# A transformer block on one core: part of VectorE's integer shifts goes to GpSimd, and two shifts become one pass

## The chip, the core and the metric

The kernel runs on one core of a Trainium2 chip. The core has a matrix engine (TensorE, PE in the profile; PEld is its weight loading), a vector engine (VectorE, DVE), an activation engine (ScalarE, ACT), a general engine (GpSimd, POOL) and a queue that issues transfers (SyncE, SP). Each engine works through its own list of instructions in order, and waits on semaphores for the others. PE writes its results to a memory of its own, PSUM; VectorE and ScalarE read PSUM, GpSimd in this kernel works on the main on-chip memory (SBUF) alone. The metric is the device time of one execution in microseconds.

## The reference

The input is one sequence of 2048 tokens of width 512, in bf16. A condition vector `c` gives six modulation vectors. Two branches follow, each with a layer norm and a residual:

```python
mod = (_silu(c) @ w_mod).reshape(c.shape[0], 6, 1, -1)
...
h = _layernorm(x) * (1 + ca) + sa
x = x + ga * attention(h, wqkv, wo)      # 32 heads of width 16, softmax over 2048 keys
h = _layernorm(x) * (1 + cb) + sb
x = x + gb * (gelu(h @ w1 + b1) @ w2 + b2)   # hidden width 1376
```

Nearly all the time is in the attention: 32 heads x 2048 x 2048 scores, of which every one has to be turned into an exponential.

## The kernel before

**Two ways to an exponential.** The queries are taken in four blocks of 512 (`QB`), the heads in four groups of eight; a run is four heads of one group for one block, and there are 32 runs (`NR`). A run has 16 key tiles of 128 keys. A unit is one head, one key tile, 512 queries: a 128 x 512 tile of scores in PSUM.

- *ScalarE's way.* `qk_a` puts three or two units (in turn) into a PSUM tile `st`, and line 847 makes the exponential of 1536 or 1024 columns into `pt` with one instruction.
- *VectorE's way.* `qk_d` computes one unit at a time into `ax`, and line 895 evicts it: it adds a constant, clamps at zero and writes a 16-bit integer into a quarter of the tile `ph` (four units: 2048 columns). Read as bf16, such an integer is already a rough exponential, piecewise linear. `shifts` (line 912) adds four further constants (`PH_SH`) to the 2048 integers, one VectorE pass each into a tile `sh` (line 915). The bf16 readings of all five, summed, approximate the exponential far better. The sum is not made: `pv_op` lets PE multiply each of the five readings with the values and add them up in PSUM (`od`), so a key tile on this way costs five such products instead of one.

In each run but the first, the key tiles 2, 6, 10 and 14 (`DKS`) are meant for VectorE; when ScalarE has finished its own tiles of a run, `next_tile` hands it what VectorE has not begun.

**Who sets the order.** All instructions are ordered by a planner (`Plan`) while the program is built. An `Op` has an engine, a duration that the planner assumes, a delay until its result can be used, a priority, operations it waits for, and a buffer it takes (`acq`, a `Res` with so many slots) or gives back (`rel`). The planner goes through time, picks for each engine what can start first, and by priority among what can start at nearly the same time. A small random number (`spread`) is added to the priority; its seed is taken from `SEEDS`, one for each 12.5 us of planned time. The order in which operations are picked is the order in each engine's list; on the chip only that order and the semaphores remain.

**GpSimd beside PSUM passes.** GpSimd multiplies the attention output with the reciprocal of its sum (`normalise`, line 1001; the sums go through SP's transfers to be spread over rows) and scales three weight tiles (`scaled`, line 1024). These are cut in two halves of 256 columns by `beside` (line 1032). The gate `plan.beside` lets such a piece start only next to a VectorE instruction that reads PSUM (`port=False`); `after_dve` makes it wait, on the chip, for the VectorE instruction ahead of that one. The flag `port=True` marks VectorE and GpSimd operations that the planner does not run at the same time.

**Start and end.** `load_x`, `load_mod` and `load_cols` issue SP's first loads: the first block of x in two halves, two modulation tiles, the first columns of the weights, which wait for the first modulation tile. `mod_columns`, `layer_norm`, `make_k`, `make_v`, `make_q` lead to the first scores. `make_q` is called ahead of need by `want_q`, with a due time. `block_tail` and `last_half` hold the output projection and the second branch of each block; the last block is done in two halves.

## Time and profile before

| | us |
|---|---|
| median of three runs | 786.2 (785.47 to 786.65) |
| the profiled execution | 786.85 |
| its span in the profile | 785.1 |
| ScalarE busy | 758.5 |
| VectorE busy | 729.0 |
| PE busy | 728.4 |
| GpSimd busy | 101.3 |
| exponentials, 632 instructions (line 847) | 716.6 |
| evictions to integers, 468 passes (line 895) | 307.7 |
| shifts, 468 passes (line 915) | 309.2 |

The clock granted to TensorE was 1.00 throughout. "Busy" counts the time in which at least one instruction of an engine was under way; successive passes of VectorE overlap by some 0.08 us in the records, so the mean duration of one (681 ns for an eviction) is longer than its share of the busy time (307.7 / 468 = 657 ns). The idle time of an engine costs nothing where another engine is the bound.

### The profile page before, as it was taken

To read this page: it belongs to the slowest core of one execution; us is meant where nothing else is said; L and a number is where in the kernel's file an instruction comes from. 1 tells how busy PE (TensorE), PEld (TensorE's weight loads), DVE (VectorE), ACT (ScalarE), POOL (GpSimd) and SP (SyncE) were. 2 spreads that over 40 slices of the span, in tenths; PEclk is the share of its full clock that TensorE was granted. 3 is DMA by queue.
4 is the path that set the end of the run, shared out by engine and by line. 5 is a ranking of instruction groups with operands and counts; after the bars stand their busy time and mean duration, and the time that the engine had idled before them with its cause. 6 is when DMAs were issued, how large, how long until landed. Compare 5 with 4: busy or idle time off the path is not lost.

```text
span 785.1 us, 20128 instructions
## 1 busy us (share of the span) xinstructions
PE 728.4 (93%) x8182; PEld 275.3 (35%) x8254; DVE 729.0 (93%) x1269; ACT 758.5 (97%) x686; POOL 101.3 (13%) x167
## 2 busy tenths in 40 slices
PE   8899999999999999999999999999888899989997
PEld 3433333333333222333233333222333444434444
DVE  6878899999999999999999999988999999999984
ACT  4999999999999999999999999999999999999994
POOL 6200103100002520010002100010001100120100
PEclk9999999999999999999999999999999999999999
DMA  7052001100011001001001010011010001000010
GB/s 215 30 168 59 18 24 43 26 15 15 15 45 49 25 19 49 18 19 44 10 20 33 24 32 7 17 33 30 25 45 24 18 18 43 20 24 18 25 44 28
DMA packets 39070, 28.19 MB, mean 36 GB/s; under 512 B 17957, under 2 KB 34374, under 8 KB 38978
## 3 DMA queue, kind: packets, MB, share of 16 engines
q1 hardware_dynamic: 38970, 26.91, 12.2%
q8 instruction: 64, 1.05, 0.6%
q14 instruction: 28, 0.23, 0.1%
q10 hardware_dynamic: 8, 0.00, 0.0%
HBM read 21.30 MB, written 2.61 MB: 30 GB/s over the span
## 4 chain that ended last, share of the span: by engine, by line
ACT 50%; PE 27%; issue 11%; DVE 10%; SPq 1%; DMA 1%; POOL 1%; POOLq 0%; DVEq 0%; ACTq 0%
ACT pt L847 47%; PE od L949 9%; PE st L798 8%; DVE sh L915 3%; DVE ph L895 3%; PE ax L1112 2%; PE ax L798 2%; ACT g L1191 1%; PE ax L1172 1%; PE ax L688 1%; SPq L716 1%; PE ax L428 1%; DVE g L1182 1%; PE t L1112 1%; PE ax L1106 0%
## 5 line engine op out<-in xcount | busy, mean ns | idle before, releaser
L847 ACT ACTIVATE pt<-st 128x1536 bf16<-128x1536 f32 x632 | 716.6, 1358 | 2.8 <-PE st L798 1.8
L895 DVE TENSOR_SCALAR ph<-ax 128x512 int16<-128x512 f32 x468 | 307.7, 681 | 15.3 <-PE ax L798 13.7
L915 DVE TENSOR_SCALAR sh<-ph 128x2048 int16<-128x2048 int16 x468 | 309.2, 691 | 2.0 <-PE od L949 1.3
L798 PE MATMUL st<-qm,kT 32*128 32x512 bf16 x1580 | 247.5, 382 | 28.9 <-ACT pt L847 22.5
L949 PE MATMUL od<-sh,VEB 128*32 128x512 bf16 (+1 forms) x2368 | 172.3, 339 | 5.4 <-DVE sh L915 3.4
L949 PEld LDWEIGHTS <-VEB 128*32 128x32 bf16 x4928 | 111.9, 95 | 161.8 <-issue 137.6
L798 PEld LDWEIGHTS <-kT 32*128 32x128 bf16 x2048 | 84.8, 91 | 235.8 <-issue 225.1
L798 PE MATMUL ax<-qm,kT 32*128 32x512 bf16 x468 | 159.8, 379 | 6.0 <-DVE ph L895 4.4
L949 PE MATMUL od<-pt,VEB 128*32 128x512 bf16 (+1 forms) x1968 | 153.6, 341 | 0.4 <-DVE OD L974 0.2
L1001 POOL TENSOR_TENSOR OT<-OD,RB 128x256 bf16<-128x256 f32 x38 | 27.9, 741 | 348.5 <-DVE sh L915 331.8
L949 PE MATMUL od<-ph,VEB 128*32 128x512 bf16 (+1 forms) x592 | 45.0, 337 | 0.0
L1172 PE MATMUL ax<-blk,W 128*128 128x512 bf16 (+1 forms) x143 | 39.5, 358 | 1.6 <-issue 0.8
L1001 POOL TENSOR_TENSOR OS<-OD,RB 128x256 bf16<-128x256 f32 x24 | 17.1, 727 | 174.8 <-DVE sh L915 154.9
L688 PE MATMUL ax<-blk,w 128*128 128x512 bf16 x100 | 32.5, 383 | 3.9 <-ACT blk L610 1.4
L1112 PE MATMUL ax<-w,g 128*128 128x512 bf16 x103 | 29.3, 381 | 1.6 <-DVE ph L895 0.8
L1182 DVE TENSOR_SCALAR g<-ax,b1c 128x512 bf16<-128x512 f32 (+1 forms) x41 | 28.3, 691 | 0.3
L594 DVE BATCH_NORM_STATS2 ln_s<-xb 128x6 f32<-128x512 bf16 x32 | 21.7, 677 | 1.2 <-DMA xb<-in_A_x_dram 1.1
L1112 PEld LDWEIGHTS <-g 128*128 128x128 bf16 x176 | 14.4, 97 | 22.3 <-issue 10.5
L974 DVE COPY OD<-od 128x512 f32<-128x512 f32 x31 | 21.2, 683 | 1.0 <-PE od L949 0.8
L1172 PEld LDWEIGHTS <-W 128*128 128x128 bf16 x176 | 13.4, 97 | 21.0 <-issue 15.5
L727 PE MATMUL ax<-w,blk 128*128 128x128 bf16 x256 | 20.3, 220 | 0.2 <-DVE ph L895 0.2
L727 PEld LDWEIGHTS <-blk 128*128 128x128 bf16 x256 | 14.8, 98 | 9.1 <-issue 8.5
(107 smaller groups left out, 331.8 us busy)
## 6 DMA issues: line engine op xcount, KB each, us to landing
RB<-rn SPq DMA_DIRECT2D x124, 64.0 KB
xb<-in_A_x_dram SPq DMA_DIRECT2D x8, 512.0 KB
out_dram<-o SPq DMA_DIRECT2D x16, 128.0 KB
qm<-qs SPq DMA_DIRECT2D x120, 16.0 KB
W<-in_B_w_dram SPq DMA_DIRECT2D x1, 1376.0 KB
w<-in_A_wqkv_dram SPq DMA_DIRECT2D x3, 384.0 KB
blk<-in_w_mod_dram SPq DMA_DIRECT2D x2, 512.0 KB
g<-in_w_mod_dram SPq DMA_DIRECT2D x2, 512.0 KB
```

Of the source, the lines that this page charges most:

```text
L594: nc.vector.bn_stats(out=st6, in_=src)
L688: return chain([(lambda ps, j=j: nc.tensor.matmul(out=ps[:, 0:QB], lhsT=w.tile[:, j, cc * P:(cc + 1) * P], rhs=o_h[b].tile[:, j, :], start ...
L727: nc.tensor.matmul(out=ps[:, t * P:(t + 1) * P], lhsT=o_h[b].tile[:, j, t * P:(t + 1) * P], rhs=o_w[2].tile[:, j, cc * P:(cc + 1) * P], st ...
L798: nc.tensor.matmul(out=o.tile[:, k * QB:(k + 1) * QB], lhsT=kT[cc][kb][rows, ko * P:(ko + 1) * P], rhs=qm.tile[rows, par, :] if hb is None ...
L847: nc.scalar.activation(out=e.tile[:, 0:len(got) * QB], in_=o.tile[:, 0:len(got) * QB], func=ACT.Exp, scale=ESC)
L895: nc.vector.tensor_scalar(out=ph.tile[:, c0:c0 + QB], in0=o.tile, scalar1=PH_B, scalar2=0.0, op0=ALU.add, op1=ALU.max)
L915: sh = op("DVE", lambda o, j=j: nc.vector.tensor_scalar(out=o.tile[:, cols], in0=first.tile[:, cols], scalar1=PH_SH[j], scalar2=None, op0= ...
L949: nc.tensor.matmul(out=o_od[r].tile[32 * i:32 * i + 32, n * HB:n * HB + w], lhsT=v_tile(kt)[:, c0:c0 + 32], rhs=got[i][:, at:at + w], star ...
L1001: two = beside(lambda c: nc.gpsimd.tensor_tensor(out=OT.tile[:, c], in0=OD.tile[:, c], in1=o5.tile[:, c], op=ALU.mult), (OT,), (OD, o5))
L1112: nc.tensor.matmul(out=ps, lhsT=g[:, f, col:col + P], rhs=rhs, start=(f == 0), stop=(f == NF - 1))
L1172: mm = chain([(lambda ps, f=f, j=j: nc.tensor.matmul(out=ps[:, 0:N], lhsT=W1[:, j, f * P:(f + 1) * P], rhs=h.tile[:, j, 0:N], start=(j == ...
L1182: ev.append(op("DVE", lambda o, f=f, mm=mm: nc.vector.tensor_scalar(out=g.tile[:, f, 0:N], in0=mm.tile[:, 0:N], scalar1=b1c[:, f:f + 1], s ...
```

## The change

- *Readings.* For a key tile on VectorE's way, `ph` now holds 4096 columns. VectorE makes the first shifted reading from the first half of `ph` into its second half (2048 columns), and then the second and third reading in one pass over the whole 4096 columns into `sh`: it adds one constant to both halves.
- *The last reading* goes to a tile of its own, `sl`. VectorE makes its first columns; up to four pieces of 256 16-bit columns are left to GpSimd, which adds a tile `step` to them as 128 32-bit integers: the constant stands in both halves of each. How many pieces, is set by a backlog: at most five pieces planned and not begun.
- *Products* that GpSimd already made are cut in four pieces of 128 columns instead of two of 256.
- *Order.* `in_turn` holds a shift back while an earlier run has shifts to do. The constants `PH_SH` are others, since the second and third reading now differ by the same constant as the first from the unshifted one. The buffers are 3 `ph` of 4096 columns, 2 `sh` of 4096, 2 `sl` of 2048 (before: 4 `ph` and 4 `sh` of 2048). The planner's duration of a piece is 0.5 instead of 0.68. Queries of the last block become due 16 units earlier. All seeds are others, and with them the order of many operations on all engines.

```diff
--- before.py
+++ after.py
@@ -23,7 +23,7 @@
 
 
 
-PH_SH = (0, 20, 43, 69, 101)
+PH_SH = (0, 24, 46, 70, 104)
 NPH = len(PH_SH)
 
 
@@ -54,7 +54,7 @@
 AL = 0.21
 FILL = 1.6
 SPREAD = 0.3
...
 HEAT = 1.45
 
 
@@ -289,7 +289,8 @@
     FEW = 1
     MM = 0.2155
     SPAN = (3, 2)
-    POOL_US, POOL_MIN = 0.68, 0.5
+    POOL_US, POOL_MIN = 0.5, 0.48
+    STEP_N, PMAX, LIMIT = 128, 4, 5
     A_US = {1: 0.475, 2: 0.904, 3: 1.33}
     AHEAD = 3
     PSUM_F = 8
@@ -313,8 +314,9 @@
     r_od = res("od", 1, [P, QB], FP32, pp)
     r_ax = res("ax", 2, [P, QB], FP32, pp)
     r_pt = [res(f"pt{n}_", NPT, [P, n * QB], BF16) for n in SPAN]
-    r_ph = res("ph", 4, [P, WIDE * 4 * QB], I16)
-    r_sh = res("sh", 4, [P, WIDE * 4 * QB], I16)
+    r_ph = res("ph", 3, [P, 2 * 4 * QB], I16)
+    r_sh = res("sh", 2, [P, 2 * 4 * QB], I16)
+    r_s4 = res("sl", 2, [P, 4 * QB], I16)
     r_xb = res("xb", 2, [P, TPB, D], BF16)
     r_blk = res("blk", NQ, [P, NC, D], BF16)
     r_w = res("w", 3, [P, NC, D], BF16)
@@ -537,6 +539,9 @@
         nc.vector.tensor_scalar(out=qmask[:, 1:2], in0=qmask[:, 1:2], scalar1=QSC, scalar2=None,
                                 op0=ALU.mult)
     o_mask = op("DVE", mask, 0.6, (o_io,), prio=0.0)
+
+    step = const.tile([P, STEP_N], I32, name="step")
+    o_step = op("POOL", lambda o: nc.gpsimd.memset(step, PH_SH[-1] * 65537), 0.2, prio=0.3)
 
     o_v0 = {}
 
@@ -700,7 +705,7 @@
             for n in range(1, 4) for p in range(2)]
 
     def make_q(b, cc, kind, acq):
-        qm = op("NIL", None, 0.0, (), lat=0.0, prio=0.0, acq=r_qm)
+        qm = op("NIL", None, 0.0, (), lat=0.0, prio=0.0 if q_left else -1.0, acq=r_qm)
         mm = proj(b, o_w[0], cc, kind, acq, after=qm)
         if (b, cc) == (0, 0):
             evs = [op("DVE", lambda o, p=p: nc.vector.tensor_scalar(
@@ -801,7 +806,7 @@
                          qm.tile[rows, :, hb * HB:(hb + 1) * HB], start=True, stop=True)
 
     def qk_deps(r, kt):
-        want_q(r // 2 + 1 if r < LAST * 8 else r - LAST * 4 + 2)
+        want_q(r // 2 + 1 if r < LAST * 8 - 2 else r - LAST * 4 + 3)
         cc, par, hb = run_heads(r)
         qm, evs = o_q[(cc, runs[r][0])]
         return [evs[par or 0], o_k[(cc, kt // TPB)]], qm
@@ -904,20 +909,60 @@
                 ph.uses -= 1
 
     live = {"A": 0, "D": 0}
+    waiting = [0] * NR
+    backlog = [0]
+
+    def in_turn(sh, r):
+        fn, sh.run = sh.fn, r
+        waiting[r] += 1
+        sh.gate = lambda: not any(waiting[:r])
+
+        def go(o):
+            waiting[r] -= 1
+            if fn is not None:
+                fn(o)
+        sh.fn = go
+        return sh
+
+    def last_shift(r, kt, first, es, acq):
+        into = in_turn(op("NIL", None, 0.0, es, lat=0.0, prio=0.0, acq=acq), r)
+        n = max(0, min(PMAX, LIMIT - backlog[0]))
+        w = 2 * STEP_N
+        cols = 4 * QB - n * w
+        parts = [in_turn(op("DVE", lambda o: nc.vector.tensor_scalar(
+            out=into.tile[:, 0:cols], in0=first.tile[:, 0:cols], scalar1=PH_SH[-1], scalar2=None,
+            op0=ALU.add), 0.06 + 0.54 * cols / (4 * QB), [into] + es, lat=DL, prio=2.0, rel=(first,), port=True), r)]
+        for i in range(n):
+            def go(o, c=slice(cols + i * w, cols + (i + 1) * w)):
+                backlog[0] -= 1
+                after_dve(nc.gpsimd.tensor_tensor(
+                    out=into.tile[:, c].bitcast(I32), in0=first.tile[:, c].bitcast(I32), in1=step, op=ALU.add))
+            backlog[0] += 1
+            parts.append(op("POOL", go, POOL_US, [into, o_step] + es, lat=0.1, prio=0.6, kind="beside", rel=(first,),
+                            port=True, gate=lambda: plan.beside(POOL_MIN)))
+        pv_op(r, kt, parts, bits(into, 0), (into,))
     d_e = []
 
     def bits(o, k):
         return lambda: [o.tile[:, h * QB:(h + 1) * QB].bitcast(BF16) for h in range(4 * k, 4 * k + 4)]
 
     def shifts(r, kts, first, es):
-        cols = slice(0, 4 * QB * len(kts))
-        for j in range(1, NPH):
-            sh = op("DVE", lambda o, j=j: nc.vector.tensor_scalar(
-                out=o.tile[:, cols], in0=first.tile[:, cols], scalar1=PH_SH[j], scalar2=None, op0=ALU.add),
-                0.06 + 0.54 * len(kts), es, lat=DL, prio=2.0, acq=r_sh, rel=(first,), port=True)
-            sh.run = r
-            for k, kt in enumerate(kts):
-                pv_op(r, kt, (sh,), bits(sh, k), (sh,))
+        kt, n = kts[0], 4 * QB
+
+        def add(j, dst, src, us, deps, acq=None):
+            o = op("DVE", lambda o: nc.vector.tensor_scalar(
+                out=dst(o), in0=src(), scalar1=PH_SH[j], scalar2=None, op0=ALU.add),
+                us, deps, lat=DL, prio=2.0, acq=acq, rel=(first,), port=True)
+            return in_turn(o, r)
+        one = op("NIL", None, 0.0, es, lat=0.0, prio=0.0)
+        a = add(1, lambda o: first.tile[:, n:2 * n], lambda: first.tile[:, 0:n], 0.6, [one])
+        b = add(2, lambda o: o.tile, lambda: first.tile, 1.14, [a], r_sh)
+        first.uses += 1
+        pv_op(r, kt, (a,), bits(first, 1), (first,))
+        first.uses -= 1
+        pv_op(r, kt, (b,), bits(b, 0), (b,))
+        pv_op(r, kt, (b,), bits(b, 1), (b,))
+        last_shift(r, kt, first, [one], r_s4)
 
     def pv_op(r, kt, deps, srcs, owners):
         cc, par, hb = run_heads(r)
@@ -1031,9 +1076,9 @@
 
     def beside(fn, deps, rel=(), prio=0.5):
 
-        return [op("POOL", lambda o, c=c: after_dve(fn(slice(c * HB, (c + 1) * HB))), POOL_US, deps, lat=0.1,
+        return [op("POOL", lambda o, c=c: after_dve(fn(slice(c * P, (c + 1) * P))), POOL_US, deps, lat=0.1,
                    prio=prio, kind="beside", rel=rel, port=True, gate=lambda: plan.beside(POOL_MIN))
-                for c in range(2)]
+                for c in range(QB // P)]
 
     def after_dve(pool):
 
@@ -1341,7 +1386,7 @@
         while q_made[0] < g and q_made[0] + 1 < NQ * NC:
             q_made[0] += 1
             b, cc = groups[q_made[0]]
-            due(32 + APR * (first_run(q_made[0]) - 1) - 32)
+            due(32 + APR * (first_run(q_made[0]) - 1) - (32 if b < LAST else 48))
             make_q(b, cc, f"q{q_made[0]}", r_ax)
             due(1e9)
             if cc == NC - 1:
```

2 lines of the change are left out of this document (1 added, 1 removed).

## The prediction

> **What bounds the kernel now.** I read the page's shares first, then its slices, then busy time by stretch of the span, then the costliest groups, the waits, and last the order of time at the start and around one GpSimd instruction. Shares and slices (PE, VectorE, ScalarE):
>
> ```profile
> PE 728.4 (93%) x8182; PEld 275.3 (35%) x8254; DVE 729.0 (93%) x1269; ACT 758.5 (97%) x686; POOL 101.3 (13%) x167
> PE   8899999999999999999999999999888899989997
> DVE  6878899999999999999999999988999999999984
> ACT  4999999999999999999999999999999999999994
> ```
>
> Three engines are above 90%, so the share alone does not say which of them sets the pace. The stretches do (columns: stretch, us, then busy us and instructions of PE, PEld, DVE, ACT, POOL, clock, DMA share, GB/s):
>
> ```profile
> 100.00:200.00 100.00, 94.24 (x1005) 33.54 (x1013) 96.88 (x167) 99.95 (x90) 14.29 (x21) 1.00 0.10 26
> 200.00:300.00 100.00, 92.80 (x983) 31.17 (x980) 98.86 (x164) 100.00 (x89) 21.59 (x32) 1.00 0.12 34
> 500.00:600.00 100.00, 90.93 (x1005) 31.86 (x1008) 90.31 (x151) 99.27 (x85) 7.23 (x9) 1.00 0.11 30
> 700.00:765.00 65.00, 62.80 (x944) 29.06 (x951) 59.62 (x106) 64.77 (x59) 7.42 (x10) 1.00 0.11 32
> ```
>
> From 100 to 765 us ScalarE is busy 99.3 to 100% of every stretch. VectorE is close behind, but is left idle 9.7 us in 500 to 600 and 5.4 us in 700 to 765. The groups and the two waits that matter (total us, times, longest):
>
> ```profile
> L847 ACT ACTIVATE pt<-st 128x1536 bf16<-128x1536 f32 x632 | 716.6, 1358 | 2.8 <-PE st L798 1.8
> L895 DVE TENSOR_SCALAR ph<-ax 128x512 int16<-128x512 f32 x468 | 307.7, 681 | 15.3 <-PE ax L798 13.7
> L915 DVE TENSOR_SCALAR sh<-ph 128x2048 int16<-128x2048 int16 x468 | 309.2, 691 | 2.0 <-PE od L949 1.3
> L1001 POOL TENSOR_TENSOR OT<-OD,RB 128x256 bf16<-128x256 f32 x38 | 27.9, 741 | 348.5 <-DVE sh L915 331.8
> ```
> ```profile
> ACT pt L847 <- PE st L798: 1.8, 4, 0.7
> DVE ph L895 <- PE ax L798: 13.7, 22, 1.9
> ```
>
> ScalarE waited for scores 1.8 us in all; VectorE waited 13.7 us for PE to give it scores. So the exponentials of ScalarE are the bound from the first to the last of them, VectorE and PE stay just ahead, and the ends of the span (before the first and after the last exponential) stand outside that bound.
>
> **The change, part by part.** The counts are from the order of the two built programs.
>
> *ScalarE.* 632 exponentials become 624, four fewer of each width, because VectorE now takes 122 key tiles instead of 117 (488 evictions for 468, four a tile). All exponentials are busy 716.6 us, or 716.6 / 316 = 2.268 us for one of each width; four such pairs are **9.1 us**, all on the path that sets the end.
>
> *VectorE's shifts.* Before: 468 passes of 2048 columns, 309.2 us, 0.661 each. After, for each of 122 tiles: one pass of 2048 (0.661), one of 4096, one of 1276 on average (55 of 1024, 29 of 1280, 24 of 1536, 13 of 1792, 1 of 2048). No row has the last two widths. The nearest narrower row is the reciprocal, 16 columns in 0.242 us. The line from it to 2048 columns gives 1.08 for 4096 and 0.50 for 1276; in proportion to the columns it is 1.32 and 0.41. I take the middle, 1.20 and 0.46: both ends treat the fixed part of a pass in an extreme way. 122 x (0.661 + 1.20 + 0.46) = 283 us (263 to 303). The 20 added evictions cost 307.7 / 468 = 0.657 each, 13.1 us. VectorE: 283 + 13 - 309 = -13 us (-33 to +7). VectorE is not the bound, so this is slack and no time.
>
> *GpSimd's pieces.* 368 adds of 128 columns are new, and the 96 products of 256 columns become 192 of 128. Nearly each of the 560 pieces is given a PSUM pass of its own to run beside; 202 of these passes are followed by a shift. What that means is seen around one product now (us from the start, length):
>
> ```profile
> 260.07 0.68 DVE L895 TENSOR_SCALAR ph<-ax 128x512 int16<-128x512 f32 x1
> 260.67 0.78 DVE L915 TENSOR_SCALAR sh<-ph 128x2048 int16<-128x2048 int16 x1
> ```
> ```profile
> 260.23 0.68 POOL L1024 TENSOR_TENSOR w<-w,gb_bc 128x256 bf16<-128x256 bf16 x1 [0.63 <-DVE sh L915]
> ```
>
> The product starts 0.16 us after its pass, and takes 0.68. The shift behind the pass starts 0.60 after it and takes 0.78 instead of the usual 0.68: it was held 0.10, and the product ended 0.24 into it. So a shift is not held by a piece that ends less than 0.14 into it: a piece of 0.60 + 0.14 - 0.16 = 0.58 us is free. The rows for a 128 x 128 add of integers: at the least half of the 0.673 of a bf16 product of 256, 0.34; at the most 0.74, no gain from half the columns. One row has 128 columns, at 5.07 us in the next list: 0.42 for a product on 4 partitions. I take 0.42, so the 560 pieces (235 us of GpSimd) lie beside their passes and hold nothing, and the pass itself is not stretched by a piece (0.68 at 260.07, as usual); at 0.74 each of the 202 shifts would be held 0.16, 32 us of VectorE. The some 4 us that products hold shifts now (mean 691 against the usual 682, 468 times) go. The Trainium skill, GPSIMD Engine Reference, section 3.1, puts a two-input add at 2.6 cycles a column and at 1.96 times VectorE's time, and section 4.1 says to leave elementwise work to VectorE; by its 4497 ns for 2048 columns 128 would be some 0.3 us plus the fixed part, an estimate. It speaks against the move only if GpSimd's time is on the path; the trace's rows, 0.42 for 128 columns and 0.74 for 256, agree with the slope, and the sum is the same by both.
>
> *PE.* 5 more tiles on VectorE's side are 96 more products with the values, four side by side, so 24 x 0.39 at most, 9 us, and 17 more warm-up products; PE has 57 us idle, 22.5 of them waiting for ScalarE's tiles. Nothing on the path, if the pieces come on time. A product with the last reading now waits for GpSimd's pieces as well as for VectorE, and behind it stand the next scores in PE's order. In GpSimd's queue the pieces also stand behind products that wait for reciprocals from SP's transfers, and behind two fills that wait for ScalarE. A VectorE eviction into a reused reading tile (3 now, 4 before) waits for the pieces that read it; in the built order these lie two or more passes back. I put **1 us** on all of this (0 to 4): ScalarE's tiles run one ahead, which hides about one pass.
>
> *The start.* The order of SP's first loads changes: before x, x, modulation, modulation; after modulation, x, modulation, x (halves of the first block of x).
>
> ```profile
> 5.07 0.42 POOL L558 TENSOR_TENSOR sr<-c_bf,ce 4x128 bf16<-4x128 bf16 x1
> 6.55 0.18 DVE L595 BATCH_NORM_AGGREGATE mv<-ln_s 128x2 f32<-128x6 f32 x1
> 8.15 0.99 DVE L605 TENSOR_SCALAR z<-xb,mv,rs 128x512 bf16<-128x512 bf16 x2 [0.61 <-POOL rs L601]
> 8.16 1.47 SPq L513 DMA_DIRECT2D w<-in_A_wqkv_dram  x3
> 9.59 0.55 PE L570 MATMUL ax<-sc,blk 128*128 128x1 bf16 x16
> 10.18 0.17 DVE L583 COPY modA<-ax 128x8 f32<-128x8 f32 x1 [1.03 <-PE ax L570]
> 15.44 1.45 ACT L847 ACTIVATE pt<-st 128x1536 bf16<-128x1536 f32 x1 [0.49 <-PE st L798]
> ```
>
> Now the four land by about 9 us: the weights wait for the first modulation load until 8.16, and the second is used at 9.59. The first normalisation is long done when the modulation columns come at 10.18. After, the second half of x lands last, at 8.2 to 9.5, and behind it stand two statistics with their closing (1.6), GpSimd's root with VectorE waiting (6.73 to 8.15, 1.4), two scalings (0.99), the transposes (some 0.7 of the 1.9 from 9.14 to 11.01, the rest being the modulation columns): 12.9 to 14.2 instead of 11.0 at the first modulation of a block, 1.9 to 3.2 us later, and the first exponential with it. Against that the weights and the next block of x are issued earlier, since their wait is for a load that is now first, and ScalarE idles 2.2 us at 23.7 for the second block's keys, some of which goes. **+1.5 us** (0 to 3).
>
> *Moved queries.* The last block's projections come due 16 units earlier; ScalarE's idle time there is under 1 us, so 0 to -0.8, taken as 0. *The end.* The last but two output tile leaves the very end, the last halves are the same work; PE is busy 9.6 of 10 us there, so 0, between -2 and +2.
>
> **Sum.** -9.1 + 1 + 1.5 = -6.6 us. The profiled execution took 786.85 us (span 785.1 and 1.75 around it), 0.65 above the median 786.2 of the three: 780.25 on its scale, **779.6** as a median.
>
> **Rivals.**
> 1. *The start costs nothing* because the loss is made up at the second block's wait, and PE is never late: -9.1, 777.1, and with the end's 2 us 775. For it: the 2.2 us idle, and the weights' earlier issue. Against it: statistics and scalings of that block stand behind the same late chain on VectorE.
> 2. *The pieces outlast their cover*, and shifts wait. VectorE has 23 us idle between 100 and 765 (3.1, 1.1, 1.0, 1.3, 9.7, 1.8, 5.4 by stretch), plus the 13 + 4 won: 40. With 6.6 of gain to lose, 46 us over 202 shifts is 0.23 each, so it decides from a piece of 0.58 + 0.23 = 0.81 us. At 0.9, 202 x 0.32 = 65 us, 25 more than the slack: 779.6 + 25 = 804. For it: no integer add is in the trace, and a power of 2 columns takes 0.824. Against it: the 128-column row. The Trainium skill, SBUF — State Buffer, section Who interferes with whom, says that whichever of the two engines comes second is blocked fully until the first ends; the held shift at 260.67 agrees.
> 3. *GpSimd's queue comes late*: each of the 31 normalisations lets pieces stand behind products that wait for a transfer; if that holds PE's product, and so the next scores, 0.5 us each time, 15 us: 795. Against it: products now start at VectorE's release, hardly ever at the transfer's.
> 4. *Nothing moves*: small losses of PE and POOL of 6 us eat the gain, 786.
>
> **How the numbers follow.** The forecast with its 776 to 783 has 0.60, the first rival 0.20, the second 0.08, the third 0.07, the fourth 0.05. So faster by over 0.2% (what this kernel's measurement can tell, 1.6 us) 0.80, the same 0.05, slower 0.15. The range leaves out the far ends of the second and third rival and the first one's last us: 775 to 788.
>
> **What would show it.** Right: 624 exponentials near 707 us busy; ScalarE still above 99% from 100 to 750; adds of 128 columns at 0.4 to 0.5 us; the 2048-wide shift back at 0.68 with hardly any longer one; first exponential at 17 to 18 us. Wrong: ScalarE waiting for PE by more than 5 us in the middle, PE for GpSimd's pieces, or shifts longer than their width.

## The result, and the profile after

The changed kernel takes **781.8 us** (median of 6 runs, 780.47 to 782.34) against 786.4 us of the kernel before beside it (6 runs); the ratio is 0.9929, with a 95% interval of 0.9909 to 0.9948. So it is faster by 0.5 to 0.9%. The profiled execution took 780.92 us (span 779.1) where the one before took 786.85 (span 785.1): 5.9 us less, predicted 6.6.

The shares and slices of the changed kernel (PE, VectorE, ScalarE):

```profile
PE 731.1 (94%) x8355; PEld 272.7 (35%) x8355; DVE 716.8 (92%) x1187; ACT 749.3 (96%) x678; POOL 284.0 (36%) x632
PE   9888999999999998999999999999999989999998
DVE  5867898999999999999999999999899999999974
ACT  2999999999999999999999999999999999999993
```

ScalarE is still the busiest, with 9 us less; VectorE has 12 us less, GpSimd nearly three times as much. Busy time in the stretches that were shown of before (us, then busy us and instructions of PE, PEld, VectorE, ScalarE, GpSimd, clock, DMA share, GB/s):

```profile
100.00:200.00 100.00, 93.27 (x999) 31.16 (x996) 96.75 (x159) 100.00 (x90) 41.67 (x91) 1.00 0.09 24
500.00:600.00 100.00, 95.65 (x1109) 33.90 (x1105) 95.14 (x149) 99.56 (x85) 32.24 (x71) 1.00 0.10 29
700.00:765.00 65.00, 63.37 (x936) 31.54 (x935) 58.34 (x103) 60.41 (x58) 20.10 (x44) 1.00 0.10 30
```

Up to 700 us ScalarE has no gap to speak of, so it is still the bound there; in the last stretch its exponentials end at 755, and it has gaps after that. The groups (total us, mean ns, idle before):

```profile
L852 ACT ACTIVATE pt<-st 128x1536 bf16<-128x1536 f32 x624 | 707.3, 1368 | 2.9 <-PE ax L803 1.3
L900 DVE TENSOR_SCALAR ph<-ax 128x512 int16<-128x512 f32 x488 | 319.8, 683 | 19.8 <-PE ax L803 17.3
L938 POOL TENSOR_TENSOR sl<-ph,step 128x128 int32<-128x128 int32 x368 | 167.9, 459 | 325.8 <-DVE sh L953 97.0
L1046 POOL TENSOR_TENSOR OT<-OD,RB 128x128 bf16<-128x128 f32 x76 | 35.3, 468 | 55.9 <-DVE sh L953 23.7
```
```profile
L953 DVE TENSOR_SCALAR sh<-ph 128x4096 int16<-128x4096 int16 x122 | 148.6, 1220 | 0.4 <-PE od L994 0.3
L953 DVE TENSOR_SCALAR ph<-ph 128x2048 int16<-128x2048 int16 x122 | 83.9, 689 | 0.5
L932 DVE TENSOR_SCALAR sl<-ph 128x1024 int16<-128x1024 int16 x55 | 23.3, 425 | 0.5 <-PE od L994 0.3
```

The reader is to see three things. There are 624 exponentials, 707.3 us busy (716.6 before). The integer piece of 128 columns takes 0.459 us, and the product of 128 columns 0.468. The shifts of one key tile are 1.22 (two readings), 0.69 (the first) and, at four pieces, 0.43 (the last): the three kinds of shift are busy 148.6 + 83.9 + 58.6 = 291.1 us where four passes a tile took 309.2, for five tiles more. (The 309.2 are one group, within which overlapping passes count once. Counted so, all shifts of the changed kernel cover 284.3 us. The runs below are compared by the sum over the kinds, as 291.1 is.) The waits that matter (total us, times, longest):

```profile
ACT pt L852 <- PE ax L803: 1.3, 2, 0.7
ACT pt L852 <- PE st L803: 1.1, 3, 0.5
```
```profile
DVE ph L900 <- PE ax L803: 17.3, 30, 2.9
```

**Where the 5.9 us are.** The stretch from the first exponential's start to the last one's end splits into the exponentials themselves and the rest (ScalarE's other work, or nothing). All of it is read from the rows of ScalarE's exponentials in the two traces:

| us | before | after | change |
|---|---|---|---|
| start of the first exponential | 15.44 | 18.58 | +3.14 |
| exponentials, busy | 716.59 | 707.34 | -9.25 |
| rest between them, up to 60 us | 6.05 | 5.39 | -0.66 |
| rest, 60 to 500 us | 7.58 | 7.61 | +0.03 |
| rest, from 500 us | 16.18 | 16.32 | +0.14 |
| from the last exponential to the end | 23.22 | 23.90 | +0.68 |
| sum: end of the last instruction | 785.06 | 779.14 | -5.92 |

The table is the whole case: the gain is the eight exponentials, and over a quarter of it (3.14 - 0.66 = 2.5 us) is given back at the start. (The last stretch, from the last exponential to the end, is called the tail below.)

The start of the changed kernel, a selection of lines in order of time (start us, length us, engine, line):

```profile
8.23 0.69 DVE L599 BATCH_NORM_STATS2 ln_s<-xb 128x6 f32<-128x512 bf16 x1 [1.37 <-DMA xb<-in_A_x_dram]
9.46 0.94 PE L575 MATMUL ax<-sc,blk 128*128 128x1 bf16 x32
10.26 0.38 PE L435 MATMUL od<-warm 128*128 128x512 bf16 x1
10.72 2.62 DVE L610 TENSOR_SCALAR z<-xb,mv,rs 128x512 bf16<-128x512 bf16 x4
11.01 3.24 POOL L550 MEMSET VEB<- 128x180 bf16 x9
...
13.30 0.38 PE L430 MATMUL ax<-warm 128*128 128x512 bf16 x1
13.52 1.05 PE L652 MATMUL st<-ident,z 128*128 128x128 bf16 x16
14.39 0.99 DVE L618 TENSOR_SCALAR blk<-st,modA 128x512 bf16<-128x512 bf16 x2 [1.06 <-PE st L652]
18.58 1.45 ACT L852 ACTIVATE pt<-st 128x1536 bf16<-128x1536 f32 x1 [0.49 <-PE st L803]
```

Here the prediction's reason does not hold as it stands. The second half of x is late (the statistics at 8.23 waited for it), but two other things end at the same time: the scalings (line 610) stand behind the modulation columns in VectorE's list and run from 10.72 to 13.34, one of the four stretched from 0.41 to 1.47 us beside GpSimd's fills from 11.01; and between the modulation products and the transposes PE's list holds 14 warm-up products, from 10.26 to 13.5, which the planner lays where PE would wait by its own times. The first experiments take these apart.

### The profile page after: what moved, and what is told of

Read it like the earlier page. It is cut to its first block, busy times and chain, and to the rows that moved or that the text cites. A ratio compares the mean times of both kernels' runs of the same rounds, so it can differ in the third digit from the quotient of the medians.

```text
span 779.1 us, 20856 instructions
## 1 busy us (share of the span) xinstructions
PE 731.1 (94%) x8355; PEld 272.7 (35%) x8355; DVE 716.8 (92%) x1187; ACT 749.3 (96%) x678; POOL 284.0 (36%) x632
## 4 chain that ended last, share of the span: by engine, by line
ACT 41%; PE 36%; DVE 12%; issue 8%; POOL 1%; DMA 1%; SPq 1%; POOLq 0%; DVEq 0%; ACTq 0%
ACT pt L852 38%; PE od L994 13%; PE st L803 10%; DVE ph L900 5%; PE ax L1157 3%; PE ax L1217 2%; PE ax L803 2%; DVE sh L953 2%; ACT g L1236 2%; PE ax L693 1%; PE ax L430 1%; DVE ph L953 1%; DVE ln_s L599 1%; DVE sl L932 1%; DVE OD L1019 1%
## 5 line engine op out<-in xcount | busy, mean ns | idle before, releaser
L852 ACT ACTIVATE pt<-st 128x1536 bf16<-128x1536 f32 x624 | 707.3, 1368 | 2.9 <-PE ax L803 1.3
L900 DVE TENSOR_SCALAR ph<-ax 128x512 int16<-128x512 f32 x488 | 319.8, 683 | 19.8 <-PE ax L803 17.3
L938 POOL TENSOR_TENSOR sl<-ph,step 128x128 int32<-128x128 int32 x368 | 167.9, 459 | 325.8 <-DVE sh L953 97.0
L994 PEld LDWEIGHTS <-VEB 128*32 128x32 bf16 x5024 | 110.5, 96 | 148.6 <-issue 125.8
L953 DVE TENSOR_SCALAR sh<-ph 128x4096 int16<-128x4096 int16 x122 | 148.6, 1220 | 0.4 <-PE od L994 0.3
L994 PE MATMUL od<-ph,VEB 128*32 128x512 bf16 (+1 forms) x1232 | 90.2, 339 | 0.6 <-DVE ph L953 0.4
L994 PE MATMUL od<-sh,VEB 128*32 128x512 bf16 (+1 forms) x1232 | 86.0, 338 | 1.6 <-DVE sh L953 1.4
L953 DVE TENSOR_SCALAR ph<-ph 128x2048 int16<-128x2048 int16 x122 | 83.9, 689 | 0.5
L932 DVE TENSOR_SCALAR sl<-ph 128x1024 int16<-128x1024 int16 (+3 forms) x122 | 58.6, 485 | 0.6 <-PE od L994 0.3
L1046 POOL TENSOR_TENSOR OT<-OD,RB 128x128 bf16<-128x128 f32 x76 | 35.3, 468 | 55.9 <-DVE sh L953 23.7
L994 PE MATMUL od<-sl,VEB 128*32 128x512 bf16 (+1 forms) x616 | 49.2, 339 | 0.6 <-DVE sl L932 0.4
L1046 POOL TENSOR_TENSOR OS<-OD,RB 128x128 bf16<-128x128 f32 x48 | 22.1, 464 | 30.3 <-DVE sh L953 13.9
```

The costliest lines, as they stand in the source:

```text
L852: nc.scalar.activation(out=e.tile[:, 0:len(got) * QB], in_=o.tile[:, 0:len(got) * QB], func=ACT.Exp, scale=ESC)
L900: nc.vector.tensor_scalar(out=ph.tile[:, c0:c0 + QB], in0=o.tile, scalar1=PH_B, scalar2=0.0, op0=ALU.add, op1=ALU.max)
L932: parts = [in_turn(op("DVE", lambda o: nc.vector.tensor_scalar(out=into.tile[:, 0:cols], in0=first.tile[:, 0:cols], scalar1=PH_SH[-1], sca ...
L938: after_dve(nc.gpsimd.tensor_tensor(out=into.tile[:, c].bitcast(I32), in0=first.tile[:, c].bitcast(I32), in1=step, op=ALU.add))
L953: o = op("DVE", lambda o: nc.vector.tensor_scalar(out=dst(o), in0=src(), scalar1=PH_SH[j], scalar2=None, op0=ALU.add), us, deps, lat=DL, p ...
L994: nc.tensor.matmul(out=o_od[r].tile[32 * i:32 * i + 32, n * HB:n * HB + w], lhsT=v_tile(kt)[:, c0:c0 + 32], rhs=got[i][:, at:at + w], star ...
```

## The experiments

Unless it says "ordered anew", an edit leaves the planner's times alone and changes only what is issued, or in which place, so that the order of all else is the changed kernel's. In every run but those of the start, the first exponential came at 18.2 to 19.2 us, so one profile does not tell smaller differences in it apart. Each ratio is to the kernel before, run beside the edited one on the same chip.

### The start: which of three things is late

**First: only the loads.** The first four loads are collected and issued in the order of the kernel before.

```diff
+    def hold(k, fn):
+        held[k] = fn
+        if len(held) == 4:
+            for i in range(4):
+                held[i]()          # x, x, modulation, modulation
...
-            first[i] = nc.sync.dma_start(out=o.tile, ...)
+            hold(2 + i, lambda: put(o))
```

> The changed kernel with its first four loads in the order of the kernel before (both halves of x, then the two modulation loads); the order on every other engine stays. Theory (the late first exponential is lost time that nothing gives back): statistics of the third tile start at 5 to 6 us instead of 8.23, the scalings still stand behind the modulation columns (10.2 us), so the first exponential starts at 16.4 to 16.8 us instead of 18.58, and the kernel takes 779.6 to 780.4 us (781.8 less 1.4 to 2.2). Rival (the loss at the start is made up at the second block's wait): the gap of 1.5 us at 26.8 grows by as much as the first exponential moves, and the time stays at 781.4 to 782.2.

Measured: 782.04 us, ratio to the kernel before 0.9936 (0.9914 to 0.9959), the same as the changed kernel's. The third tile's statistics did start at 5.89 us, but the first exponential came at 18.37 us, 0.2 earlier and not 2, and within the spread of runs whose start is unchanged. The transposes on PE still started at 13.30. Both the theory and its rival fall: nothing was made up later, because nothing was won. x's second half alone does not set the start.

**Second: only the warm-up products.** A flag leaves out the products that PE makes to stay busy, between the last modulation product and the first transpose.

```diff
+        if not warmer and (n, m) == (1, NC - 1):
+            quiet[0] = True              # after the modulation products
...
+                        quiet[0] = False # at the first transpose
...
-        return Op("PE", lambda o: nc.tensor.matmul(
+        return Op("PE", hot(lambda o: nc.tensor.matmul(   # nothing while quiet
```

> The changed kernel without the 14 warm-up products that stand on PE between the modulation columns (10.26 us) and the first transposes (13.52 us). Theory (at the start three things end together: these 14 x 0.217 = 3.0 us of PE's order, the second half of x, and VectorE's scalings behind the modulation columns): the scalings still end at 12.3 to 13.3 us, so the first exponential comes at 17.4 to 18.5 instead of 18.58, and the time is 780.8 to 781.8 us. Rival (the warm-up products alone hold the start): first exponential at 16 to 17 us, 779.4 to 780.4 us.

Measured: 784.09 us, ratio 0.9965 (0.9953 to 0.9976), **slower** than the changed kernel (781.8, and 780.9 in a later run) by 2 to 3 us, which neither theory had. The first exponential came at 19.69; 0.5 us of that are x's second half, which landed later here. PE's rows and the stretches, in which the clock is the third number from the end, show why:

```profile
8.08 0.95 PE L580 MATMUL ax<-sc,blk 128*128 128x1 bf16 x32
...
13.51 1.78 PE L660 MATMUL st<-ident,z 128*128 128x128 bf16 x15 [1.09 <-DVE z L617]
15.51 0.63 PE L435 MATMUL ax<-warm 128*128 128x512 bf16 x1 [0.22 <-PE st L660]
```
```profile
10.00:11.00 1.00, 0.00 (x0) 0.00 (x0) 0.93 (x5) 0.00 (x0) 0.35 (x2) 0.81 0.94 316
...
15.00:16.00 1.00, 0.78 (x5) 0.45 (x5) 1.00 (x3) 0.52 (x1) 0.00 (x0) 0.50 0.97 310
```

With nothing on PE for 3.1 us the granted clock falls to 0.50 at 10.6 us (0.81 is the mean of 10 to 11) and stays there until some 17.4; a warm-up product of 512 columns takes 0.63 us instead of 0.38, and the 15 last transposes 1.78 instead of 1.05 for 16. The Trainium skill, TensorE: Matmul & The Clock Gate, section HAM oscillation — how this bites in real kernels, asks for no idle gap on PE over some 3.4 us. The clock here fell after 0.95 us of one-column products and about 1.6 us of nothing, and the whole gap was 3.1 us, so that this trace asks for more than the rule. The later start is 1.1 us of the 3.2 by which the two profiles differ; 0.9 us are gaps between exponentials from 60 to 500 us, where the clock fell once more (at 133.5 us), and 0.8 us lie in the tail.

**Third: all three.** Loads as in the first run, the modulation columns' copy issued behind a scaling, and no warm-up product there.

```diff
+        def after_z(o):
+            later_mod.append(lambda: out_(o))
-        return op("DVE", out_, 0.4, (mm,), ...)
+        return op("DVE", out_ if warmer else after_z, 0.4, (mm,), ...)
...
+        if t == TPB - 1 and later_mod:   # in apply(), the scaling
+            later_mod.pop()()
```

> The changed kernel with all three undone: both halves of x loaded first, the scalings ahead of the modulation columns on VectorE, and no warm-up products ahead of the transposes. Theory (the start costs 2.5 us net, and all three must go): transposes right behind the modulation columns at 10.2 to 10.4 us, first exponential at 15.3 to 15.9 us; of the 2.7 to 3.3 us some 0.65 are given back at the second block's wait, so 779.1 to 779.8 us. Rival (what is won at the start is waited for at the second block's keys): first exponential as early, the gap near 24 to 27 us grows by 2 us or more, 781.3 to 782 us.

Measured: 781.38 us, ratio 0.9932 (0.9913 to 0.9951); first exponential at 16.90, 1.7 us earlier and not 3. Two things spoiled it. The planner happened to put the fourth tile's scaling first, so three scalings still stood behind the modulation columns. And PE, idle for 0.4 and 0.8 us, was again granted half the clock:

```profile
10.49 2.16 PE L677 MATMUL st<-ident,z 128*128 128x128 bf16 x16 [0.80 <-DVE z L632]
```
```profile
10.00:11.00 1.00, 0.39 (x4) 0.26 (x5) 1.00 (x4) 0.00 (x0) 0.99 (x5) 1.00 1.05 341
11.00:12.00 1.00, 0.96 (x11) 0.70 (x10) 0.56 (x1) 0.00 (x0) 0.76 (x3) 0.54 1.05 339
```

**Fourth: mended.** The copy now waits for all four scalings, and the first three of the 14 warm-up products stay (the records show two of the three).

```diff
-        if t == TPB - 1 and later_mod:
+        z_done[0] += 1
+        if z_done[0] == TPB:
             later_mod.pop()()
...
+            if quiet[0]:
+                quiet[0] += 1
+            if quiet[0] < 5:      # three warm-up products are kept
+                put(o)
```

> The changed kernel with x's halves loaded first, all four scalings ahead of the modulation columns on VectorE, and 3 of the 14 warm-up products kept between the modulation columns and the transposes, so that PE is not idle there. Theory (the run without any of the 14 lost half of its gain to the granted clock, 0.93 in the first 25 us, with transposes of 2.16 us instead of 1.05): clock 1.00 in the first 25 us, transposes from 10.5 us in 1.05, first exponential at 15.6 to 16.3 us, 2.3 to 3 us earlier than 18.58, and the time 1.8 to 2.6 us under that of the changed kernel run beside it. Rival (the clock falls whatever stands on PE, as it did once in the run of the end's edit): 0.9 to 0.95 and a first exponential near 16.9.

The changed kernel was run once more on the same chip beside it:

> The changed kernel once more, beside the version with the mended start. Every theory expects 780.5 to 783 us and a ratio of 0.992 to 0.995 to the kernel before.

Measured: **779.39 us** (778.43 to 780.29), ratio to the kernel before 0.990 (0.9871 to 0.9929); the changed kernel beside it 780.9 us (780.5 to 782.75), ratio 0.9922 (0.9893 to 0.9952). By the medians the mended start is worth 1.5 us. Their intervals against the kernel before overlap, but the highest of its six times is below the lowest of the changed kernel's six, and the executions with a mean clock of 1.00 alone differ by 1.6 us (medians 779.21 and 780.85). It is the fastest version of this study.

```profile
8.77 2.14 DVE L637 TENSOR_SCALAR z<-xb,mv,rs 128x512 bf16<-128x512 bf16 x3 [0.61 <-POOL rs L633]
...
10.53 0.38 PE L445 MATMUL od<-warm 128*128 128x512 bf16 x1
10.75 1.05 PE L683 MATMUL st<-ident,z 128*128 128x128 bf16 x16
...
15.88 1.45 ACT L883 ACTIVATE pt<-st 128x1536 bf16<-128x1536 f32 x1 [0.49 <-PE st L834]
```
```profile
0.00:25.00 25.00, 20.44 (x167) 10.20 (x169) 18.31 (x46) 12.45 (x15) 13.55 (x40) 1.00 0.61 189
```

The clock is 1.00, the transposes take 1.05 us and start 2.8 us earlier than in the changed kernel, and the first exponential starts 2.7 us earlier. Of these 2.7 us 1.2 are lost again in this profile behind 500 us, at 604 us (a wait of 1.39 for the changed kernel's 0.71, of which more below) and at 625 (0.61, none in the changed kernel).

### The end

The four products of the last but one run no longer wait for a VectorE pass each, and the last load of x goes ahead of that run's transfers.

```diff
-        return [op("POOL", lambda o, c=c: after_dve(fn(...)), POOL_US, ...
+        put = after or after_dve      # nothing for r == NR - 2
+        return [op("POOL", lambda o, c=c: put(fn(...)), POOL_US, ...
...
             nc.sync.dma_start(out=o.tile, in_=x_src[b])
+            while late_shift:
+                late_shift.pop()()    # the transfers of run NR - 2
```

> The changed kernel with two things of the end undone: the four output products of the last but one run no longer wait for a VectorE pass each, and the last load of x is issued ahead of the four transfers of that run. Theory (the end lost 2 us before the first residual add, of which the fourth product's wait is 1.0 and x's late landing 0.4): the transfers are issued near 753.4 instead of 754.06 and the add at 760.22 comes 1.0 to 1.9 us earlier, and the kernel with it: 779.9 to 780.8 us. Rival (PE's products with the second weights, 759.7 to 764.3, set the end, so that the add only waits elsewhere): the add comes earlier, the last output stays, 781.5 to 782.1 us.

Measured: 782.67 us, ratio 0.9931 (0.9906 to 0.9955): no change. The transfers were issued 2.25 us ahead of the last exponential's end, where the changed kernel has 1.18; yet the residual add came only 0.42 us earlier after that end (4.56 for 4.98), and the tail is 23.74 us for 23.90. Here is what ends the wait for the add, first in the changed kernel, then in this run:

```profile
760.22 0.69 DVE L1301 TENSOR_TENSOR xb<-t,xb 128x512 bf16<-128x512 f32 x1 [2.60 <-DMA xb<-in_A_x_dram]
```
```profile
762.49 0.69 DVE L1311 TENSOR_TENSOR xb<-t,xb 128x512 bf16<-128x512 f32 x1 [2.19 <-ACT g L1241]
```

The wait for x is gone and another takes its place. PE's rows of the changed kernel show it:

```profile
755.63 0.61 PE L1217 MATMUL t<-blk,W 128*128 128x256 bf16 x4
...
757.82 1.46 PE L1151 MATMUL t<-Wo,OT 128*128 128x512 bf16 x6
```

PE's list has sixteen products with the first weights (line 1217) and two with the second ahead of those with `Wo`, and they run from 755.63 to 757.82 without a pause. The view names ScalarE's first GELU, on which the products with the second weights depend, but PE's products do not pause for it. In the kernel before the products with `Wo` came first, 0.4 us after the last exponential; in the changed kernel they come 2.6 us after it (757.82 for 755.24), and in this run, with its earlier transfers, 2.6 us too. So the rival holds in substance, with PE's order in place of PE's load. What removing this order would win was not tried.

### The count of exponentials

VectorE's tiles are capped at 117, as many as before; the rest is ordered anew, and came out much the same up to 700 us.

```diff
+    d_left = [117]
+
     def d_job():
+        if d_left[0] == 0:
+            return NR, 0
```

> The changed kernel with VectorE's key tiles held at 117, as many as in the kernel before, so 632 exponentials again; the pieces, the merged pass and the start stay, and the rest is ordered anew. Theory (the gain is the eight exponentials and nothing else): 8 x 1.134 = 9.1 us more, 790 to 792 us, ScalarE over 99% busy from 100 to 750 us and VectorE with some 24 us more idle. Rival (the new readings shorten waits as well): under 788 us.

Measured: 790.22 us, ratio 1.0047 (1.0031 to 1.0063): 8 to 9 us more than the changed kernel, and slower than the kernel before. The stretch from first to last exponential is 745.52 us against 736.66, 8.9 more. VectorE has no tiles left at the end, and 21 of 50 us idle while ScalarE is full:

```profile
L856 ACT ACTIVATE pt<-st 128x1536 bf16<-128x1536 f32 x632 | 716.5, 1371 | 2.6 <-PE ax L807 1.2
```
```profile
700.00:750.00 50.00, 46.29 (x641) 21.75 (x645) 28.99 (x51) 49.99 (x45) 12.61 (x27) 1.00 0.09 25
```

The theory holds: the time follows the count of exponentials, and all else that the change does to VectorE is worth nothing by itself. This run has the changed kernel's seeds, constants and buffers too, so these alone do not win time either. Its profiled execution is 2.0 us longer than that of the kernel before (787.1 for 785.1), and the later start (18.35 - 15.44 - 0.66 = 2.25) accounts for that; the medians differ by 3.6 us, and what the rest of that is stays open.

### What the pieces are worth

GpSimd's integer adds are taken out and VectorE makes the whole last reading, in the same order.

```diff
-            out=into.tile[:, 0:cols], in0=first.tile[:, 0:cols], scalar1=PH_SH[-1], ...
+            out=into.tile, in0=first.tile[:, 0:4 * QB], scalar1=PH_SH[-1], ...
...
-                after_dve(nc.gpsimd.tensor_tensor(
-                    out=into.tile[:, c].bitcast(I32), in0=..., in1=step, op=ALU.add))
```

> The changed kernel with all of GpSimd's integer adds taken out and VectorE making the whole last reading, order of all else as in the changed kernel. Theory (the pieces win VectorE's slack, which is what lets it have 122 tiles): 122 passes of 2048 columns in place of 1276 on average cost 0.61 - 0.40 = 0.21 us each from start to start, 26 us, against some 19 us that VectorE idles between 25 and 755 us; idle before VectorE's passes falls to under 6 us, ScalarE waits for scores by 4 to 12 us, and the time is 786 to 794 us. Rival (VectorE has slack enough with 122 tiles even alone, and the merged pass is what counts): 781 to 783 us.

Measured: 795.1 us (791.39 to 799.72), ratio 1.0098 (1.0062 to 1.0135); the expected 786 to 794 was a little low. In the execution with a mean clock of 0.999 the span is 789.6, 10.5 us over the changed kernel's at that clock; in the others, at 0.986 to 0.991, it is 793.1 to 797.9, and whether the waits lower the clock or the clock makes the waits is open. VectorE's shifts are busy 316.1 us instead of 291.1. The chain of work that ended last, by engine, of the changed kernel and of this run, and this run's last reading and exponentials:

```profile
ACT 41%; PE 36%; DVE 12%; issue 8%; POOL 1%; DMA 1%; SPq 1%; POOLq 0%; DVEq 0%; ACTq 0%
```
```profile
DVE 51%; PE 23%; ACT 13%; issue 6%; DMA 3%; SPq 2%; POOL 1%; DVEq 0%; POOLq 0%; ACTq 0%
L852 ACT ACTIVATE pt<-st 128x1536 bf16<-128x1536 f32 x624 | 713.6, 1273 | 15.3 <-PE ax L803 8.0
L932 DVE TENSOR_SCALAR sl<-ph 128x2048 int16<-128x2048 int16 x122 | 83.4, 689 | 0.4 <-PE od L992 0.2
```

The bound has moved: VectorE leads the chain, and ScalarE waits 15.3 us (2.9 in the changed kernel). So the pieces win 25 us of VectorE, and these are what lets it have 122 tiles: without them the same 122 tiles make the kernel 1.0% slower than the kernel before with its 117.

### What the merged pass is worth

Each pass over 4096 columns is made as two of 2048.

```diff
+                for c in range(0, to.shape[1], n):
-            nc.vector.tensor_scalar(out=dst(o), in0=src(), scalar1=PH_SH[j], ...
+                    nc.vector.tensor_scalar(out=to[:, c:c + n], in0=of[:, c:c + n], ...
```

> The changed kernel with each merged pass of 4096 columns made as two of 2048, the order of all else kept. Theory (the merged pass saves 2 x 0.61 - 1.13 = 0.09 us from start to start, 122 times 11 us, and VectorE idles some 19 us between 25 and 755): most of it fits into VectorE's idle time, 782 to 786 us, ScalarE waiting 1 to 4 us more in the middle. Rival (VectorE has nothing to spare, each us of it is a us of the whole): 791 to 794 us.

Measured: 781.99 us, ratio 0.9934 (0.9914 to 0.9953); the changed kernel beside it has 0.9922. VectorE's shifts are busy 298.6 us for 291.1, 7.5 more, and about 1 us of it reaches the time by the medians (781.99 for 780.9), which the overlapping intervals do not make certain. As expected, most lies in VectorE's idle time. Together with the run before: the first 7 us of VectorE cost 1 at most, the first 25 cost 10 to 14. So in this order the pieces are what carries the five tiles, and the merged pass adds little.

The merged pass without any pieces, ordered anew, was also run:

```diff
-    STEP_N, PMAX, LIMIT = 128, 4, 5
+    STEP_N, PMAX, LIMIT = 128, 0, 5
```

> The changed kernel without any integer adds on GpSimd, ordered anew for it: the two readings in one pass alone. This order has 639 exponentials. Theory (the time follows ScalarE's count): 15 exponentials more than the changed kernel, 15 x 1.134 = 17 us, 797 to 801 us, slower than the kernel before, so the merged pass alone does not bring the five tiles. Rival (the merged pass carries the gain and GpSimd little): 781 to 786 us.

Measured: 809.51 us, ratio 1.0289 (1.0264 to 1.0313), 28 us over the changed kernel where the count of exponentials gives 17. In its own order VectorE is busy only 81.3 of 100 us from 100 to 200 and ScalarE 94.6, so the new order is worse than its count; why was not looked into. It shows that the merged pass alone does not bring the tiles in this planner, and no more.

### Pieces that outlast their cover

Each integer add is followed by a second one on spare data, with no wait and no reader.

```diff
                 after_dve(nc.gpsimd.tensor_tensor(... in1=step, op=ALU.add))
+                nc.gpsimd.tensor_tensor(out=spare, in0=step, in1=step, op=ALU.add)
```

> The changed kernel with each of GpSimd's 368 integer adds followed by another of the same size on spare data, with no wait and no reader: GpSimd is held 0.92 us instead of 0.46 beside a pass of 0.60. Theory (VectorE's four-times-speed passes cannot start while GpSimd works, but PSUM passes can): those of the adds that are followed by a shift (some 130 to 200) hold it 0.3 to 0.5 us each, 45 to 90 us, of which VectorE's slack takes up to 20; 805 to 850 us, mean duration of a 4096-column or 2048-column pass visibly longer (over 0.75 for 2048). Rival (GpSimd's length does not touch VectorE as long as nobody waits for the result): 781 to 784 us, passes as long as now (0.689 and 1.220).

Measured: 802.49 us (one run): less than the theory's 805 to 850, far from the rival.

```profile
L941 POOL TENSOR_TENSOR spare<-step 128x128 int32<-128x128 int32 x368 | 208.9, 568 | 0.0
L939 POOL TENSOR_TENSOR sl<-ph,step 128x128 int32<-128x128 int32 x368 | 176.8, 480 | 196.5 <-DVE sh L955 59.3 <-DVE ph L955 51.1 <-DVE sl L933 33.6
L955 DVE TENSOR_SCALAR sh<-ph 128x4096 int16<-128x4096 int16 x122 | 156.8, 1288 | 0.4 <-PE od L996 0.2
L955 DVE TENSOR_SCALAR ph<-ph 128x2048 int16<-128x2048 int16 x122 | 90.1, 739 | 0.5
```

VectorE's shifts are busy 156.8 + 90.1 + 66.6 (the last reading, all its widths) = 313.5 us, 22.4 more, and the time rises by about as much (at a mean clock of 0.991), since VectorE leads the chain again (48% for ScalarE's 11%). The holding is real, but smaller than expected, because it goes both ways. The second add starts some 0.6 us after the pass at the earliest, just as a shift would, and whoever is first keeps the other waiting. Of the 368 second adds 93 begin during a shift; they take 1.04 us on average and end after it, while the other 275 take 0.41. The other way round, 162 of the 366 shifts begin with more than 0.15 us of a piece of GpSimd's still to go; they are 23.8 us longer in all than the rest of their widths, some 0.15 each where the theory had 0.3 to 0.5. The Trainium skill, SBUF — State Buffer, section Who interferes with whom, says that issue order decides who blocks; the trace agrees, in both directions.

### The products

The products of GpSimd are made in pieces of 256 columns again, in every other place.

```diff
-        return [op("POOL", lambda o, c=c: after_dve(fn(slice(c * P, (c + 1) * P))), ...
+        return [op("POOL", lambda o, c=c: after_dve(fn(slice((c - 1) * P, (c + 1) * P))) if c % 2 else None, ...
```

> The changed kernel with the products back in pieces of 256 columns (96 instead of 192), every other piece's place kept. Theory (a 256-column product of 0.68 to 0.74 us outlasts its pass and holds the VectorE pass behind it by 0.1 us, 40 to 60 times): VectorE's passes between int16 tiles busy 2 to 5 us more than 291.1 in all, taken from its idle time, and the time is as the changed kernel's, 780.5 to 782.5 us. Rival (VectorE's 4 us are 4 us of the whole): 784 to 786 us.

Measured: 782.32 us, ratio 0.995 (0.9934 to 0.9967). VectorE's shifts are busy 295.5 us, 4.4 more, and the time is that of the changed kernel or a little over it (0.9929). As expected.

## Why the prediction was right, step by step

*Exponentials, -9.1.* Measured -9.25, and the cap at 117 tiles gives the same from the other side, 8.9. The step carries the case.

*The readings.* 1.20, 0.46 and 0.661 us were taken for the three passes of a tile; 148.6 / 122 = 1.218, 58.6 / 122 = 0.480 and 83.9 / 122 = 0.688 were measured. The middle between the two ways of scaling was close: all shifts together cover 284.3 us, where the prediction had 283. The 0.661 was read from passes that often followed each other and overlapped by 0.08 us in the records; a first shift now stands alone between others, and the rows are not quite alike. VectorE's busy time fell by 12.2 us, predicted 13.

*The piece, 0.42, free up to 0.58.* Measured 0.459, so it lies under the bound. In the trace it starts 0.16 us after its pass and ends as the shift begins; this is one of the new products (first VectorE, then GpSimd):

```profile
267.88 0.68 DVE L900 TENSOR_SCALAR ph<-ax 128x512 int16<-128x512 f32 x1
268.47 1.22 DVE L953 TENSOR_SCALAR sh<-ph 128x4096 int16<-128x4096 int16 x1
```
```profile
268.04 0.46 POOL L1046 TENSOR_TENSOR OS<-OD,RB 128x128 bf16<-128x128 f32 x1 [0.17 <-DVE ph L900]
```

The shift at 268.47 takes 1.22 us, as any. That the pieces hold nothing is nearly so: 12 of the 366 shifts begin with more than 0.14 us of such a piece still to go, and they are longer than usual by 1.65 us in all. The bound itself was not tried with a piece close to 0.58. That the holding of some 4 us by the products would go was right (4.4 in the run with 256 columns).

*Stalls, +1.* Measured +0.17 in the profiled execution (0.03 and 0.14 in the table). One place shows the mechanism: at 606 us ScalarE waited 0.71 us (1.76 in the second profile of the same kernel) for scores that waited for queries.

```profile
595.64 2.41 SPq L1056 DMA_DIRECT2D OT<-OS  x4
...
598.77 1.78 SPq L721 DMA_DIRECT2D qm<-qs  x3
...
601.23 3.69 SPq L721 DMA_DIRECT2D qm<-qs  x5
```
```profile
604.95 0.39 PE L803 MATMUL ax<-qm,kT 32*128 32x512 bf16 x1 [0.83 <-DMA qm<-qs]
```

The eight transfers of one projection stand in SP's list behind the four of an output and among those of a denominator; they end at 604.9, and PE waits 0.83 us for them. That place belongs to the step *moved queries*, taken as 0: it is 0 to some 1 us. It is also where the mended start lost part of its gain (1.39 us of waiting there). In the second profile, with its 1.76 us, the granted clock fell to 0.50 at the same place, from 606.1 to 609.5 us.

*The start, +1.5.* The sum was mis-sized and its reason incomplete. Measured: the first exponential +3.14, of which 0.66 come back at the second block, so +2.5, which lies in the range of 0 to 3. The prediction's chain gave 1.9 to 3.2 us for the first exponential, and 3.14 lies in that too, but this is in part luck: the late half of x was the only cause in it, and undoing that alone won 0.2 us, no more than the spread. The sign that it named, a first exponential at 17 to 18 us, was missed (18.58). What the prediction did not look at is the order that stands around the late load: scalings behind the modulation columns, beside GpSimd's fills, and 14 warm-up products ahead of the transposes. These two were to be seen in the order of the built program. Undoing the loads alone or the warm-up products alone won no time, and undoing all three, with three warm-up products kept, won 2.7 us at the first exponential; the scalings alone, and pairs, were not run.

*The end, 0 (-2 to +2).* Measured +0.68: about 2 us lost ahead of the first residual add (4.98 us after the last exponential for 2.93), some 1.6 by PE's order and 0.4 by x's later landing, of which 1.5 are won back by the block's output tile, which stood behind the last one before (781.61 after 780.15) and no longer does.

*The sum.* -9.25 + 0.17 - 0.66 + 3.14 + 0.68 = -5.92 against -6.6. That it came so close is partly luck: the start and the end were 1.0 and 0.7 us larger than forecast, and the stalls 0.8 us smaller. On the scale of medians the forecast was 779.6 and the result 781.8; 1.5 of these 2.2 us are the scale: the execution before that was profiled lay 0.65 over its median, the one after 0.89 under it.

*The rivals.* That the start costs nothing: no, it cost 2.5. That pieces outlast their cover: not at 0.46, and the run with doubled adds shows what it would have been, with the lock as told but less holding, since a second add that comes after the shift's start waits itself. That GpSimd's queue comes late: PE waited 0.2 us for pieces in all. That nothing moves: no.

## What to carry to other kernels

Where one engine is the bound and another makes the same thing by another way, count what moves between them: eight instructions of 1.13 us explain this gain, and 25 us of helping work by a third engine count only through them. When an early transfer is late, look at what the order built around it does with the gap, and undo all that ends at the same time before judging any of it. Warm-up work on an engine has a price in its list, but taking it all out can cost more than it holds.

## What was not expected of the hardware

- *The granted clock of PE can halve within some 3 us of little work.* It fell to 0.50 at about 10.6 and 11.1 us in the two runs without warm-up products there, in the latter after 32 one-column products and gaps of 0.4 and 0.8 us; it came back 6.8 and 3.4 us later. With three warm-up products kept between the modulation products and the transposes it stayed at 1.00 in the profiled execution. Every fall ahead of the tail, in all the traces of this study, lasted 3.4, 6.8 or 10.2 us.
- *The time of an execution goes with the granted clock.* Spans of the kernel before were 783.5 to 785.5 us where the mean granted clock was 1.00 or 0.999, 786.9 at 0.995 and 792.2 at 0.983: some 4.5 us for each hundredth. One place shows how. In the run with only the loads undone the clock fell at 131.9 us for 3.4 us, and ScalarE then waited 0.87 us for scores at 134.2; in the changed kernel's profile, at the same place of the same order, PE was as busy before (2.85 of 3.40 us), the clock did not fall and ScalarE did not wait. Why it falls in one execution and not in another is open. Kernels that differ by under 2 us are better compared at the same clock.
- *A VectorE scaling took three times as long amid GpSimd's fills.* In the changed kernel one scaling of 512 bf16 columns takes 1.47 us where its neighbours take 0.41: it runs from 11.52 to 12.99, amid fills of `VEB` whose records follow each other with hardly a gap from 11.39 on. The mended start has the same 1.47, the kernel before, in which most fills come behind the scalings, 0.58 at most. That the fills hold it is read from these times alone; no run moved the fills.
- *The same exponentials are busy longer when more of them have to wait.* The 624 exponentials cover 707.3 us in the changed kernel and 713.6 in the one without pieces, which has more gaps between them. Each record is shorter there (a mean of 1273 ns for 1368), but the records overlap less.
